# Linear attention and a gated feed-forward block: first queries in 1 KB runs, the sums of batch 0's second half behind the first half-units, batch 1's squares shared between two engines, and the steady groups' sums in consecutive units

## The chip, the cores and the metric

The kernel runs on one core of one Trainium2 chip. The metric is device time in microseconds (us). The time of an execution is about 2 us more than the span of its profile (325.02 us against a span of 323.1 us for the profiled run of the kernel before).

Names of the engines in the profile: PE is TensorE (matrix products), PEld its weight loads, DVE is VectorE, ACT is ScalarE, POOL is GpSimd, SP is SyncE, which here only issues DMAs. "SPq" and "ACTq" are those engines' sequencers.

## The reference, cut to what matters

```python
# q, k, v: [8 batches, 8 heads, 576 rows, 64], float32
kv  = einsum('bhsd,bhse->bhde', k, v)           # 64 x 64 state of each head
out = einsum('bhsd,bhde->bhse', q, kv)
out = out / sqrt(mean(out*out, -1) + 1e-6) * g_norm
x   = out.transpose(0, 2, 1, 3).reshape(4608, 512)
xn  = x / sqrt(mean(x*x, -1) + 1e-6) * rms_g
y   = (silu(xn @ w_gate) * (xn @ w_val)) @ w_out   # 512 -> 1536 -> 512
```

Both norms are folded into one scale per row and head, "alpha", made of two sums over the squares of a head: a plain one and one weighted by the square of `g_norm`.

## The kernel before

Batch by batch, 512 rows of each batch form a group: 12 "up" units (a gate product, a value product, SiLU, multiplication), then the "down" products. The last 64 rows of all eight batches form a ninth group. While PE runs one group's feed-forward, the next batch's attention is slipped in between the units. The order on each engine is the program's order.

Batch 0 has no predecessor to hide behind. It is done in two halves of 256 rows, called A and Z: load queries, cast, turn (transpose) on PE, column products, squares, sums, root, scaling, turn, and then the first up units, in half and quarter sizes:

```python
def load_q0(f, hs, queue):                       # f: half of the 512 rows
    src = q[0, hs, 256*f : 256*f+256, :].rearrange("h (p t) d -> p h (t d)", t=2)   # runs of 512 B
    queue.dma_start(out=q0[:, f, hs, :], in_=src)

def put_q0(f, ps, half, engine):                 # turned queries, PSUM -> SBUF
    js = slice(2*half, 2*half+2)
    cast(engine, qt0[:, js, 256*f : 256*f+256], ps[:, js].rearrange("p j i t -> p j (i t)"))
...
    A.sums()
    oA = rows_of(A)
    cast_q0(1, hs0, DVE)
    cast_q0(1, hs1, GP)
    A.head()
    qps = turn_q0(1, 0)
    A.root_by_table(lambda: put_q0(1, qps, 0, DVE))
    put_q0(1, qps, 1, SC)
    ...                                          # block 0 weights rounded, Z's columns and squares
    xs = [A.scale(c, oA[c]) for c in range(2)]
    x_turn(A, 0, xs[0], DVE)
    x_turn(A, 1, xs[1], DVE)
    Z.alloc_sums()
    Z.sums()

    ffn = Ffn(0)
    first = ffn.pair_banks()
    for lo in (0, 128):
        for u in range(2):
            ffn.half_unit(first[0], u, wg_sb, u, lo, lo + 128)
    oZ = rows_of(Z)
    for u in range(2):
        ffn.half_unit(first[1], u, wv_sb, u, 0, 256)
    Z.head()
    Z.root_by_table(lambda: round_w(1, "g", 2, DVE))
    ...
    xs = [Z.scale(c, oZ[c]) for c in range(2)]
    for s, engine in enumerate((GP, SC, DVE, DVE)):
        round_w(1, "v", s, engine)               # "rounding": scale a weight slice, write it as bf16
    SC.preload_act_table(ACT.Silu)
    clear_tail_rows(0, GP)                       # two memsets of 64 x 512
```

Batch 1 takes its sums from squares of columns, and batches 2 to 7 spread theirs over the steps of the running group:

```python
def f_cols(j):
    ...
    F.turned(j, ps)
    SC.activation(out=F.sq[:, j, :], in_=ps, func=ACT.Square)

# steady groups: step u runs after up unit u of group n
kv0, os = (2, (4, 5, 7, 8)) if n == 1 else (0, (2, 4, 6, 7))
for c, u in enumerate(os):
    steps[u].append(lambda a=a, c=c: a.o(c))           # products, squares
    steps[u + 1].append(lambda a=a, c=c: a.sums(c))    # VectorE
late = int(n == 1)
steps[9 + late]  += [a.head]
steps[10 + late] += [a.guess]
steps[11] += [a.root]
for c in range(T):
    steps[11] += [lambda a=a, c=c: a.scale(c), lambda a=a, c=c: a.x_rows(c)]  # x_rows: DMA transpose
```

## Time and profile before

| | |
|---|---|
| time | 325.02 us median of 3 runs (324.85 to 325.19) |
| PE busy | 315.9 us of a span of 323.1 us |
| one 512-column product | 216 ns from start to start |
| PE stretches with waits | 0 to 22 us, 40.2 us (0.18 us, which the prediction did not list), 48.8 us, 122.3 us |

The page of the kernel before, its line of busy times (us, share of the span, instructions) and the line of the chain that ended last, by engine:

```profile
PE 315.9 (98%) x1925; PEld 156.8 (49%) x1925; DVE 180.9 (56%) x370; ACT 178.1 (55%) x318; POOL 21.2 (7%) x44
...
PE 85%; DMA 7%; DVE 4%; SPq 1%; ACT 1%; issue 1%; DVEq 0%
```

PE is full except at the start and in a few short waits. The chain of waits of the kernel before for its first 50 us shows what the start is made of. Columns: start in us, length in us, what.

```profile
1.64 6.53 DMA st<-in_q_dram
...
9.30 9.27 DMA st<-in_moe_w_gate_dram
...
18.59 0.35 DVE wg_sb L203
18.95 0.17 DVE Zal L449
...
19.21 1.29 DVE xna L453 x2
20.50 0.90 DVE wv_sb L203 x2
...
21.45 0.72 PE v_ps L489 x5
```

The load of the first queries, then the load of the second block of gate weights, then VectorE: a rounding, the reciprocal that ends Z's root (`Zal`), two scalings, two roundings, for which PE waits. The timeline of the kernel before shows that last wait. Columns: start, length, engine, line, operation, out<-in, shape, count, and in brackets the idle time before.

```profile
20.42 0.97 DVE L203 TENSOR_SCALAR wv_sb<-st,rowscale 128x256 bf16<-128x256 f32 x2
20.70 0.55 POOL L280 MEMSET kb<- 64x512 bf16 x1
20.79 0.49 PE L489 MATMUL v_ps<-xnt,wv_sb 128*128 128x256 bf16 x3
21.18 0.67 POOL L280 MEMSET vb<- 64x512 bf16 x1
21.45 0.72 PE L489 MATMUL v_ps<-xnt,wv_sb 128*128 128x256 bf16 x5 [0.17 <-DVE wv_sb L203]
```

From the third to the fourth of these products 440 ns pass instead of 109: 0.33 us lost. The two roundings together take 0.97 us.

Batch 1's sums in the timeline of the kernel before:

```profile
48.37 0.62 ACT L856 ACTIVATE sqt<-v_ps 128x512 bf16<-128x512 f32 x1
...
48.52 0.78 PE L419 MATMUL att_ps<-sel,sqt 128*128 128x4 bf16 x16
49.04 0.17 PEld L419 LDWEIGHTS <-sqt 128*128 128x128 bf16 x4 [0.17 <-ACT sqt L856]
```

The last four sums wait for ScalarE's last square; by the starts of the products, 0.22 us are lost. The third group's border in the timeline of the kernel before:

```profile
114.69 5.17 SPq L385 DMA_TRANSPOSE xnt<-xna  x4
...
122.79 1.03 PE L472 MATMUL g_ps<-xnt,wg_sb 128*128 128x512 bf16 x4 [0.25 <-DMA xnt<-xna]
```

The four transposes of the next x are issued from 114.69 us on; the last one, issued at 118.63 us, lands at 122.75, and 0.41 us are lost by the starts of the products.

### The profile page before, as it was taken

To read this page: it belongs to the slowest core of one execution; us is meant where nothing else is said; L and a number is where in the kernel's file an instruction comes from. 1 tells how busy PE (TensorE), PEld (TensorE's weight loads), DVE (VectorE), ACT (ScalarE), POOL (GpSimd) and SP (SyncE) were. 2 spreads that over 40 slices of the span, in tenths; PEclk is the share of its full clock that TensorE was granted. 3 is DMA by queue.
4 is the path that set the end of the run, shared out by engine and by line. 5 is a ranking of instruction groups with operands and counts; after the bars stand their busy time and mean duration, and the time that the engine had idled before them with its cause. 6 is when DMAs were issued, how large, how long until landed. Compare 5 with 4: busy or idle time off the path is not lost.

```text
span 323.1 us, 5133 instructions
## 1 busy us (share of the span) xinstructions
PE 315.9 (98%) x1925; PEld 156.8 (49%) x1925; DVE 180.9 (56%) x370; ACT 178.1 (55%) x318; POOL 21.2 (7%) x44
## 2 busy tenths in 40 slices
PE   8899999999999999999999999999999999999995
PEld 3585455554454444444544454444544444444443
DVE  4786747569437942785268615870588058803410
ACT  3586547666756575557665765666554355223321
POOL 1263252100000000000000000000000000000000
PEclk9999999999999999999999999999999999999999
DMA  7999999994379556942794279956101620050014
GB/s 258 349 350 386 379 373 290 258 295 127 65 193 291 137 66 178 309 134 51 193 307 134 48 148 201 314 140 162 66 2 26 152 83 0 18 169 12 0 35 97
DMA packets 75125, 54.87 MB, mean 170 GB/s; under 512 B 42200, under 2 KB 68060, under 8 KB 75100
## 3 DMA queue, kind: packets, MB, share of 16 engines
q1 hardware_dynamic: 74720, 53.88, 59.5%
q10 hardware_dynamic: 380, 0.66, 0.6%
q8 instruction: 15, 0.25, 0.3%
q14 instruction: 10, 0.08, 0.1%
HBM read 37.75 MB, written 9.44 MB: 146 GB/s over the span
## 4 chain that ended last, share of the span: by engine, by line
PE 85%; DMA 7%; DVE 4%; SPq 1%; ACT 1%; issue 1%; DVEq 0%
PE g_ps L472 27%; PE v_ps L472 27%; PE o_ps L516 23%; DMA st<-in_moe_w_gate_dram 3%; PE att_ps L272 2%; DMA st<-in_q_dram 2%; PE att_ps L343 2%; DMA xnt<-xna 1%; DVE h_sb L478 1%; DVE xna L378 1%; PE g_ps L516 1%; PE v_ps L516 1%; DMA out_dram<-o_sb 1%; ACT sqt L856 1%; SPq L385 1%
## 5 line engine op out<-in xcount | busy, mean ns | idle before, releaser
L478 DVE TENSOR_TENSOR h_sb<-silu,v_ps 128x512 bf16<-128x512 bf16 x104 | 71.1, 683 | 109.8 <-PE v_ps L472 72.7
L472 PE MATMUL g_ps<-xnt,wg_sb 128*128 128x512 bf16 x416 | 106.8, 380 | 0.2 <-DMA xnt<-xna 0.2
L472 PE MATMUL v_ps<-xnt,wv_sb 128*128 128x512 bf16 x416 | 106.8, 379 | 0.0
L477 ACT ACTIVATE silu<-g_ps 128x512 bf16<-128x512 f32 x104 | 62.6, 602 | 63.4 <-PE g_ps L472 55.4
L516 PE MATMUL o_ps<-wo_sb,h_sb 128*128 128x512 bf16 x396 | 87.5, 379 | 0.0
L472 PEld LDWEIGHTS <-wv_sb 128*128 128x128 bf16 x416 | 40.7, 98 | 49.1
L516 PEld LDWEIGHTS <-h_sb 128*128 128x128 bf16 x420 | 40.7, 98 | 47.8 <-issue 0.2
L472 PEld LDWEIGHTS <-wg_sb 128*128 128x128 bf16 x416 | 38.6, 98 | 40.5 <-DMA xnt<-xna 0.7
L106 ACT COPY o_sb<-o_ps 128x512 f32<-128x512 f32 (+1 forms) x34 | 19.7, 580 | 38.1 <-PE o_ps L516 37.3
L361 DVE TENSOR_REDUCE ssq<-sq 128x16 f32<-128x1024 bf16 x28 | 34.2, 1220 | 1.0
L352 ACT ACTIVATE sq<-att_ps 128x512 bf16<-128x512 f32 x28 | 16.7, 597 | 13.7 <-PE att_ps L343 8.7
L106 ACT CAST vb<-st 128x512 bf16<-128x512 f32 (+2 forms) x33 | 18.9, 625 | 5.2 <-DMA st<-in_v_dram 5.2
L378 DVE TENSOR_TENSOR xna<-outa,s1y 128x512 bf16<-128x512 bf16 x28 | 17.5, 686 | 0.2
L106 ACT CAST qb<-st 128x1024 bf16<-128x1024 f32 (+1 forms) x15 | 14.2, 987 | 3.8 <-DMA st<-in_q_dram 3.8
L354 ACT CAST outa<-att_ps 128x512 bf16<-128x512 f32 x28 | 16.3, 581 | 0.0
L106 ACT CAST kb<-st 128x512 bf16<-128x512 f32 (+1 forms) x25 | 14.0, 619 | 0.0
L360 DVE TENSOR_TENSOR sq<-sq,gsq 128x512 bf16<-128x512 bf16 x28 | 11.7, 419 | 0.0
L343 PEld LDWEIGHTS <-qt 128*128 128x128 bf16 x96 | 7.4, 98 | 5.7
L343 PE MATMUL att_ps<-kv_all,qt 128*128 128x128 bf16 x96 | 9.3, 219 | 0.0
L272 PEld LDWEIGHTS <-kb 128*128 128x128 bf16 x120 | 7.7, 98 | 2.8
L613 PE MATMUL att_ps<-kv_all 128*128 128x512 bf16 (+1 forms) x21 | 7.5, 486 | 1.2 <-DVE sel L602 1.2
L272 PE MATMUL att_ps<-vb,kb 128*128 128x128 bf16 x120 | 8.7, 219 | 0.0
(137 smaller groups left out, 167.2 us busy)
## 6 DMA issues: line engine op xcount, KB each, us to landing
out_dram<-o_sb SPq DMA_DIRECT2D x16, 512.0 KB, 3.0
st<-in_q_dram SPq DMA_DIRECT2D x7, 1024.0 KB, 7.2
st<-in_k_dram SPq DMA_DIRECT2D x6, 1024.0 KB, 10.3
st<-in_v_dram SPq DMA_DIRECT2D x6, 1024.0 KB, 10.9
st<-in_moe_w_out_dram SPq DMA_DIRECT2D x6, 512.0 KB, 12.2
st<-in_moe_w_gate_dram SPq DMA_DIRECT2D x4, 512.0 KB, 9.3
st<-in_moe_w_val_dram SPq DMA_DIRECT2D x4, 512.0 KB, 9.9
st<-in_k_dram SPq DMA_DIRECT2D x4, 288.0 KB, 5.1
```

Source lines behind the costliest of these rows:

```text
L106: engine.copy(out=dst, in_=src)
L272: PE.matmul(ps, lhsT=bufs[b]["k"][:, t, hs, :], rhs=bufs[b]["v"][:, t, hs, :], start=(first and t == 0), stop=(last and t == T),)
L343: PE.matmul(cols, lhsT=self.qt[:, j, 128 * c : 128 * c + 128], rhs=kv_all[:, self.n, j, :], start=(j == 0), stop=(j == NS - 1),)
L352: SC.activation(out=self.sq[c][:, 0], in_=ps, func=ACT.Square)
L354: SC.copy(out=self.outa[c], in_=ps)
L360: DVE.tensor_tensor(out=sq[:, 1], in0=sq[:, 0], in1=gsq8, op=OP.mult)
L361: DVE.reduce_sum(out=self.ssq[:, c], in_=sq, axis=AX.X)
L378: DVE.tensor_tensor(out=self.xna[c], in0=self.outa[c], in1=self.alpha[:, c, :].to_broadcast([128, H, D]), op=OP.mult)
L472: PE.matmul(ps, lhsT=wt[:, s, j * 128 : (j + 1) * 128], rhs=x[:, s, :], start=(s == 0), stop=(s == NS - 1),)
L477: SC.activation(out=silu, in_=g_ps, func=ACT.Silu)
L478: DVE.tensor_tensor(out=self.h[:, j, :], in0=silu, in1=v_ps, op=OP.mult)
L516: PE.matmul(self.o_ps[c], lhsT=self.h[:, j, c * 128 : (c + 1) * 128], rhs=wo_sb[:, j, :], start=(j == 0), stop=(j == NF - 1),)
```

## The change

The intent: fewer, longer transfers for the first queries, so that batch 0 starts sooner; the squares of batch 1 off ScalarE's critical piece; and x of the steady groups ready one or two units sooner. A partition now takes 4 rows of 4 heads in 1,024 B runs, alternate partitions holding the two groups of heads; copies with a stride of 2 separate them after the turn, both of them on ScalarE for the second half. Besides, the sums of Z, which stood in front of the first half-units of the feed-forward, now stand behind the first two of them. The rows of batch 0 therefore leave in another order, in four DMAs instead of two.

```diff
+            elif c % 2 == 1 and n == 0:
+                r0 = 256 * (c // 2)
+                rows = out[r0 : r0 + 256, :].rearrange("(p c t) d -> t p c d", c=2, t=2)
+                for t in range(2):
+                    nc.sync.dma_start(out=rows[t], in_=self.o_sb[64 * t : 64 * t + 64])
...
-    def load_q0(f, hs, queue):
-        src = q[0, hs, 256 * f : 256 * f + 256, :].rearrange("h (p t) d -> p h (t d)", t=2)
-        queue.dma_start(out=q0[:, f, hs, :], in_=src)
+    def load_q0(f, queue):
+        dst = q0[:, f].rearrange("(p g) h x -> p g h x", g=2)
+        for g in range(2):
+            src = q[0, 4 * g : 4 * g + 4, 256 * f : 256 * f + 256, :].rearrange("h (p t) d -> p h (t d)", t=4)
+            queue.dma_start(out=dst[:, g], in_=src)
...
+        return ps.rearrange("p j t (x g) -> p j t x g", g=2)
+    def put_q0(f, ps, g, engine):
+        dst = qt0[:, 2 * g : 2 * g + 2, 256 * f : 256 * f + 256].rearrange("p j (t x) -> p j t x", t=4)
+        cast(engine, dst, ps[:, :, :, :, g])
...
-    A.root_by_table(lambda: put_q0(1, qps, 0, DVE))
-    put_q0(1, qps, 1, SC)
+    A.root_by_table(lambda: None)
+    for g in range(2):
+        put_q0(1, qps, g, SC)
...
-    Z.alloc_sums()
-    Z.sums()
     ffn = Ffn(0)
     first = ffn.pair_banks()
+    Z.alloc_sums()
     for lo in (0, 128):
         for u in range(2):
             ffn.half_unit(first[0], u, wg_sb, u, lo, lo + 128)
+        if lo == 0:
+            Z.sums()
...
-        SC.activation(out=F.sq[:, j, :], in_=ps, func=ACT.Square)
+        if j == 1:
+            copy = osb_pool.tile([128, 2, d_model], FP32, name="o_sb")[:, 0, :]
+            DVE.tensor_copy(out=copy, in_=ps)
+            DVE.tensor_tensor(out=F.sq[:, j, :], in0=copy, in1=ps, op=OP.mult)
+        else:
+            SC.activation(out=F.sq[:, j, :], in_=ps, func=ACT.Square)
...
     att1.kv_copy()
+    clear_tail_rows(1, DVE)
+    for i, engine in enumerate((DVE, SC, DVE, GP)):
+        cast_q(1, slice(2 * i, 2 * i + 2), engine)       # both stood elsewhere before
...
-            kv0, os = (2, (4, 5, 7, 8)) if n == 1 else (0, (2, 4, 6, 7))
+            kv0, os = (2, (4, 5, 7, 8)) if n == 1 else (0, (2, 3, 5, 6))
...
-            late = int(n == 1)
-            steps[9 + late] += [a.head]
-            steps[10 + late] += [a.guess]
-            steps[11] += [a.root]
+            late = 2 * int(n == 1)
+            steps[8 + late] += [a.head]
+            steps[9 + late] += [a.guess, a.root]
             for c in range(T):
-                steps[11] += [...]
+                steps[10 if c == 0 and not late else 11] += [...]
```

More of the change, by code (lines that the diff above doesn't have):

```diff
@@ L531, in down_out @@
                     )
-            elif c % 2 == 1:
-                if n == 0:
-                    r0 = 256 * (c // 2)
-                    rows = out[r0 : r0 + 256, :].rearrange("(p t) d -> p t d", t=2)
-                else:
-                    rows = out[n * S : n * S + MAIN, :].rearrange("(p t) d -> p t d", t=T)[:, c - 1 : c + 1, :]
+            elif c % 2 == 1 and n == 0:
[3 more added lines that the diff above has]
+                    nc.sync.dma_start(out=rows[t], in_=self.o_sb[64 * t : 64 * t + 64])
+            elif c % 2 == 1:
+                rows = out[n * S : n * S + MAIN, :].rearrange("(p t) d -> p t d", t=T)[:, c - 1 : c + 1, :]
                 nc.sync.dma_start(out=rows, in_=self.o_sb)
@@ L573 @@
         alloc_kv(0, name)
-    q0 = stage().rearrange("p (f h x) -> p f h x", f=2, h=H)
-    def load_q0(f, hs, queue):
-        src = q[0, hs, 256 * f : 256 * f + 256, :].rearrange("h (p t) d -> p h (t d)", t=2)
-        queue.dma_start(out=q0[:, f, hs, :], in_=src)
+    q0 = stage().rearrange("p (f h x) -> p f h x", f=2, h=H // 2)
+    def load_q0(f, queue):
[3 more added lines that the diff above has]
+            queue.dma_start(out=dst[:, g], in_=src)
     for j in (0, 1):
@@ L588 @@
     )
-    load_q0(0, slice(0, 8), nc.sync)
+    load_q0(0, nc.sync)
     for j in (2, 3):
@@ L592 @@
         load_kv(0, "v", nc.sync, slice(j, j + 1))
-    load_q0(1, slice(0, 8), nc.sync)
+    load_q0(1, nc.sync)
     for blk in range(2):
@@ L623 @@
     Z = Cols(0, 256, 512, qt0, sqt0, "Z")
+    qb0 = qb0.rearrange("p t h d -> p (t h d)").rearrange("p (f t h d) -> p f t h d", f=2, t=4, h=4)
     def cast_q0(f, hs, engine):
-        cast(engine, qb0[:, 2 * f : 2 * f + 2, hs, :], q0[:, f, hs, :].rearrange("p h (t d) -> p t h d", t=2))
+        cast(engine, qb0[:, f, :, hs, :], q0[:, f, hs, :].rearrange("p h (t d) -> p t h d", t=4))
     def turn_q0(f, dummies):
@@ L630, in turn_q0 @@
         warm(bank, dummies)
-        ps = bank.bitcast(BF16).rearrange("p (j i t) -> p j i t", j=NS, i=2)
-        for j in range(NS):
-            for i in range(2):
+        ps = bank.bitcast(BF16).rearrange("p (j t x) -> p j t x", j=2, t=4)
+        for j in range(2):
+            for t in range(4):
                 PE.matmul(
-                    ps[:, j, i, :], lhsT=qb0[:, 2 * f + i, 2 * j : 2 * j + 2, :], rhs=identity,
-                    is_transpose=True, start=(i == 0 and j == 0), stop=(i == 1 and j == NS - 1),
-                )
-        return ps
-    def put_q0(f, ps, half, engine):
-        js = slice(2 * half, 2 * half + 2)
-        cast(engine, qt0[:, js, 256 * f : 256 * f + 256], ps[:, js].rearrange("p j i t -> p j (i t)"))
+                    ps[:, j, t, :], lhsT=qb0[:, f, t, 2 * j : 2 * j + 2, :], rhs=identity,
+                    is_transpose=True, start=(j == 0 and t == 0), stop=(j == 1 and t == 3),
+                )
+        return ps.rearrange("p j t (x g) -> p j t x g", g=2)
+    def put_q0(f, ps, g, engine):
+        dst = qt0[:, 2 * g : 2 * g + 2, 256 * f : 256 * f + 256].rearrange("p j (t x) -> p j t x", t=4)
+        cast(engine, dst, ps[:, :, :, :, g])
     def state0(j, dummies):
@@ L678, in rows_of @@
         return banks
-    hs0, hs1 = slice(0, 4), slice(4, 8)
+    hs0, hs1 = slice(0, 2), slice(2, 4)
     warm_ps = att_pool.tile([128, 512], FP32, name="att_ps")
@@ L693 @@
     put_state0(1, kv1)
+    banksA = [gps_pool.tile([128, MAIN], FP32, name="g_ps"), vps_pool.tile([128, MAIN], FP32, name="v_ps")]
     qps = turn_q0(0, 2)
@@ L706 @@
     cast_kv(0, "v", 3, DVE)
-    banksA = [gps_pool.tile([128, MAIN], FP32, name="g_ps"), vps_pool.tile([128, MAIN], FP32, name="v_ps")]
     columns(A, 0, banksA[0])
@@ L729 @@
     A.head()
+    banksZ = [gps_pool.tile([128, MAIN], FP32, name="g_ps"), vps_pool.tile([128, MAIN], FP32, name="v_ps")]
     qps = turn_q0(1, 0)
-    A.root_by_table(lambda: put_q0(1, qps, 0, DVE))
-    put_q0(1, qps, 1, SC)
+    A.root_by_table(lambda: None)
+    for g in range(2):
+        put_q0(1, qps, g, SC)
     for name in ("g", "v"):
@@ L736 @@
                 round_w(0, name, s, GP)
-    banksZ = [gps_pool.tile([128, MAIN], FP32, name="g_ps"), vps_pool.tile([128, MAIN], FP32, name="v_ps")]
     warm(banksZ[0], 2)
@@ L847 @@
         round_wo(0, i, 1, engine)
-    for i, engine in enumerate((DVE, SC, DVE, GP)):
-        cast_q(1, slice(2 * i, 2 * i + 2), engine)
     alloc_xnt(1)
@@ L882 @@
             round_wo(blk, i, 1, GP)
-    clear_tail_rows(1, GP)
     F = Cols(1, 0, 512, turns.qt, sqt_pool.tile([128, NS, MAIN], BF16, name="sqt"), "F")
@@ L967 @@
                 steps[u + 1].append(lambda a=a, c=c: a.sums(c))
-            late = int(n == 1)
-            steps[9 + late] += [a.head]
-            steps[10 + late] += [a.guess]
-            steps[11] += [a.root]
+            late = 2 * int(n == 1)
+            steps[8 + late] += [a.head]
+            steps[9 + late] += [a.guess, a.root]
             for c in range(T):
-                steps[11] += [lambda a=a, c=c: a.scale(c), lambda a=a, c=c: a.x_rows(c)]
+                steps[10 if c == 0 and not late else 11] += [lambda a=a, c=c: a.scale(c), lambda a=a, c=c: a.x_rows(c)]
         b = n + 2
```

## The prediction

> **What bounds it.** TensorE: the page has PE busy for 315.9 of 323.1 us at full clock, and the table of stretches 20.00 of 20.00 us almost everywhere after 60 us; a 512-column product takes 216 ns. The change keeps every TensorE instruction, so it can win only PE idle time. By the starts of consecutive products in the timeline that lies in three places:
> - 0 to 22 us. The chain of waits: the query load (1.64 to 8.17 us), the gate-weight load (9.30 to 18.57), VectorE work behind it, the last value-weight rounding, for which PE waits 0.33 us at 21.0. DMA share: 0.98 in the first 20 us, 1.06 in the next.
> - Batch 1's sums at 48.8 us: 0.22 us for ScalarE's last of four column squares (597 ns each).
> - The border at 122.3 us: 0.4 us, until the group's last transposed x tile lands (122.75). Other borders lose under 0.1.
>
> **Costs and gains.**
> 1. Query load. Packets: 512 B take about 29 ns, 1,024 B about 51. Estimate: 2,048 small packets are 59 us of engine time, 1,024 larger ones 52; over 16 engines 0.4 us less. The Trainium skill (DMA: Bandwidth & Descriptors, Specifications) gives 512 B as the least transfer for line rate; this trace disagrees (17.6 against 20 B/ns per engine). The extra issues also hold the second half until the first has landed, so v's last piece (11.22 us) competes with less. The load stream up to 43 us moves 0.4 us forward.
> 2. Strided copies. VectorE's copy of a turned half was 0.42 us. The Trainium skill (VectorE: DVE Perf Modes, What auto-detection actually checks) wants 16-bit operands at step 1 for the fast mode; at step 2 I expect 0.68 us, as 512 fp32 elements from PSUM take here. ScalarE stays at 0.58. Off the critical path: the last pair's k and v products end later.
> 3. Z's sums later: no PE work saved. A's chain may come 0.6 us forward; Z's root still waits for weights and VectorE, so 0.4 is left at 21.5 us.
> 4. Batch 1: VectorE takes one column's copy and product (about 0.68 us each) while idle. Wins 0.2. Clearing tail rows and later query casts hide behind the query load landing at 43.17 us; that has 0.3 us to spare, so PE cannot come much further forward than the loads.
> 5. Steady groups: head, guess and root one to two units earlier from batch 3 on. PE is full; VectorE (11 of 20 us) has room. Only the 122.3 us border wins, 0.4. Batch 2's border at 89.2 us stays just in time.
> 6. Batch 0's output in four issues, not two: transposes of batch 2's queries about 0.4 us later, with 0.8 to spare.
>
> **Prediction.** 0.4 + 0.2 + 0.4, about 1.0 to 1.1 us less: **323.9 us**, 80% range 323.0 to 324.8. Faster by over 2%: 0.01; within 2%: 0.98; slower by over 2%: 0.01.
>
> **What would show it.** First query half landing at 7.5 to 7.9 us instead of 8.18, the last v piece by 10.7; first full-width up product at about 25.4 instead of 25.9; no wait before batch 1's sums; no gap at the third border; strided VectorE copy near 0.68 us.
>
> **What would make it wrong.** Loads into every other partition slower than 20 B/ns; the load pace past 20 us not following, so that PE waits at batch 1's query turn (gain only 0.5); the first stage gaining its whole 0.6 us or more (gain 1.5); a new wait at the 89 us border; VectorE's longer runs of sums holding up an up unit.

## The result, and the profile after

| | changed kernel | kernel before | ratio, 95% interval |
|---|---|---|---|
| first measurement | 324.70 us (324.46 to 324.87, 4 runs) | 325.11 us (324.85 to 325.56, 4 runs) | 0.9985 [0.9968, 1.0003] |
| again, another chip | 324.62 us (323.99 to 325.01, 6 runs) | 325.25 us (324.89 to 325.86, 11 runs) | 0.9975 [0.9963, 0.9987] |

A ratio is the mean time of one kernel's fast runs over that of the other's of the same rounds, so not quite the ratio of the medians quoted beside it. The gain is 0.4 to 0.6 us where 1.0 to 1.1 was forecast: the time is inside the forecast range, but the gain is about half of what the terms add up to, and the interval of the first measurement still holds 1.

The page of the changed kernel, the same two lines:

```profile
PE 316.0 (98%) x1925; PEld 156.5 (49%) x1925; DVE 181.5 (56%) x373; ACT 178.3 (55%) x318; POOL 20.3 (6%) x42
...
PE 92%; DMA 4%; DVE 2%; SPq 0%; ACT 0%; issue 0%; DVEq 0%
```

To see where the time came from, I lay the two traces side by side at five points, each the start of one instruction in the timeline (us):

| point | before | after | difference | second pair: before, after, difference |
|---|---|---|---|---|
| scaling of A's rows starts | 15.15 | 14.81 | -0.34 | 15.73, 15.02, -0.71 |
| first SiLU of a full-width unit | 26.89 | 27.21 | +0.32 | 27.12, 27.60, +0.48 |
| first SiLU of group 1 | 57.26 | 57.16 | -0.10 | 57.50, 57.76, +0.26 |
| first SiLU of group 4 | 157.61 | 157.11 | -0.50 | 157.78, 157.72, -0.06 |
| end of the span | 323.06 | 322.65 | -0.41 | 323.17, 323.21, +0.04 |

The second pair is a slower-than-usual execution of the changed kernel (325.01 us, the slowest of its six) against a usual one of before (325.15), so its end is no measure of the gain; its course is what matters. In both pairs the changed kernel comes earlier into A's scaling and **later** out of the first stage. It then wins back what it lost at other places. In the first pair these are 0.18 us at a hold at 40.2 us that the changed kernel happened not to have (its second profile has it), 0.22 us at batch 1's sums and 0.41 us at the third border; in the second pair 0.22 and 0.24 us.

The chain of waits of the changed kernel, first 30 us:

```profile
1.64 5.06 DMA st<-in_q_dram
...
7.37 5.50 DMA st<-in_q_dram
...
12.97 0.43 DVE qb L108
13.40 0.18 DVE Ar L224
...
17.66 0.27 DVE Zr L224
...
18.53 0.35 DVE wg_sb L203
18.88 0.20 DVE Zal L449
...
19.17 1.29 DVE xna L453 x2
20.46 0.99 DVE wv_sb L203
...
21.50 0.99 PE v_ps L489 x6
```

The two parts of the first query half land at 6.70 and 7.44 us (before, the whole at 8.18), and those of the second half are issued at 6.72 and 7.37. A's sums run at 12.41 us instead of 13.18, but A's head (`Ar`) stands in VectorE's order behind the cast of the second query half (12.97 us), so only 0.31 of these 0.77 us remain: 13.31 instead of 13.62. Then Z's chain begins (`Zr`, its first reciprocal) at 17.66 instead of 17.35 us. In the chain of before, the load of the second gate block (landing at 18.57 us) ended last, and VectorE's rounding of it (`wg_sb`) followed at 18.59. Here this load lands at 18.18 us, but VectorE, busy with Z's chain, comes to the rounding only at 18.45, so at the end of Z's root (`Zal`) 0.04 us is left of the load's 0.39: 18.82 instead of 18.86 in the timelines. And the last rounding stands there with 0.99 us alone. The timeline of the changed kernel at that place:

```profile
20.30 0.52 POOL L280 MEMSET kb<- 64x512 bf16 x1
20.38 1.33 DVE L203 TENSOR_SCALAR wv_sb<-st,rowscale 128x256 bf16<-128x256 f32 x2
20.75 0.38 PE L489 MATMUL v_ps<-xnt,wv_sb 128*128 128x256 bf16 x2
20.76 0.53 POOL L280 MEMSET vb<- 64x512 bf16 x1
...
21.50 0.99 PE L489 MATMUL v_ps<-xnt,wv_sb 128*128 128x256 bf16 x6 [0.36 <-DVE wv_sb L203]
```

The single records of the two roundings are 1,060 and 347 ns. The first began 0.08 us after the first memset and ended 0.15 us after the second one. PE loses 0.53 us before its third product and 0.16 before its fourth, where before it lost 0.33.

Batch 1's sums in the timeline of the changed kernel run through without a wait (0.55 us for the sixteen, before 0.78); VectorE's copy and product take 0.69 us each:

```profile
47.99 0.69 DVE L864 TENSOR_TENSOR sqt<-o_sb,att_ps 128x512 bf16<-128x512 f32 x1
48.02 0.60 ACT L866 ACTIVATE sqt<-v_ps 128x512 bf16<-128x512 f32 x1
...
48.64 0.55 PE L419 MATMUL att_ps<-sel,sqt 128*128 128x4 bf16 x16
```

At the third border of the changed kernel the transposes go out 1.83 us sooner and PE does not wait:

```profile
112.86 5.16 SPq L385 DMA_TRANSPOSE xnt<-xna  x4
...
122.30 1.03 PE L472 MATMUL g_ps<-xnt,wg_sb 128*128 128x512 bf16 x4
```

### The profile page after: what moved, and what is told of

It reads as the page before. It is cut to its first block, busy times and chain, and to the rows that moved or that the text cites. A ratio compares the mean times of both kernels' runs of the same rounds, so it can differ in the third digit from the quotient of the medians.

```text
span 322.7 us, 5143 instructions
## 1 busy us (share of the span) xinstructions
PE 316.0 (98%) x1925; PEld 156.5 (49%) x1925; DVE 181.5 (56%) x373; ACT 178.3 (55%) x318; POOL 20.3 (6%) x42
## 4 chain that ended last, share of the span: by engine, by line
PE 92%; DMA 4%; DVE 2%; SPq 0%; ACT 0%; issue 0%; DVEq 0%
PE g_ps L472 28%; PE v_ps L472 28%; PE o_ps L516 27%; DMA st<-in_q_dram 3%; PE att_ps L272 2%; PE att_ps L343 2%; PE v_ps L516 1%; PE g_ps L516 1%; DVE xna L453 1%; DMA out_dram<-o_sb 1%; PE v_ps L489 1%; PE o_ps L489 1%; PE g_ps L489 0%; PE att_ps L338 0%; PE att_ps L285 0%; PE att_ps L265 0%
## 5 line engine op out<-in xcount | busy, mean ns | idle before, releaser
L360 DVE TENSOR_TENSOR sq<-sq,gsq 128x512 bf16<-128x512 bf16 x28 | 11.7, 418 | 0.0
## 6 DMA issues: line engine op xcount, KB each, us to landing
st<-in_moe_w_out_dram SPq DMA_DIRECT2D x6, 512.0 KB, 11.4
```

Source lines behind the costliest of these rows:

```text
L360: DVE.tensor_tensor(out=sq[:, 1], in0=sq[:, 0], in1=gsq8, op=OP.mult)
```

## The experiments

Two theories stood for the loss in the first stage. **P**: GpSimd's two memsets of batch 0's tail rows, which now begin just as VectorE's last roundings do, hold these roundings up. **Z**: Z's sums, now behind the first half-units, start Z's root, scaling and roundings too late. All kernels below gave correct results. Times are against the kernel before in the same rounds.

Because loads land at other times in each execution (in the nine profiles of kernels that share the changed kernel's code up to Z's sums, the second gate block landed between 17.46 and 19.28 us), single profiles are compared by two things that need no common clock: the length of the two roundings, and the stretch from the start of A's scaling to the first SiLU of a full-width unit. I collect them here from the records:

```
kernel              roundings (ns)   PE gaps (us)   stretch (us)
before               365   689       0.33            11.74
before_again         345   697       -               11.39
after               1060   347       0.53 + 0.16     12.40
after_again          366   689       0.33            12.58
late_clear           421   333       -               11.70
double_clear         872   690       0.34 + 0.50     12.51
z_sums_first         345   692       -               11.43
z_late               366   337       -               11.27
z_late_cast          346   348       -               11.29
before_late_clear    362   334       -               11.66
before_z_later      1231   346       0.70 + 0.16     12.47
query_only           365   347       -               11.22
undo_f               344   575       0.19            11.86
undo_steady          448   333       -               11.73
```

(PE gaps: time beyond the usual 109 ns from one product to the next within the second pair's eight value products, where it is over 0.15 us.)

Two things stand in these rows beside the theories. First, the memsets are not alone: the 421, 448 and 575 ns of late_clear, undo_steady and undo_f overlap no memset but a weight rounding that GpSimd does itself (20.93 to 21.41, 21.11 to 21.59 and 21.05 to 21.68 us), and end 0.14 to 0.15 us after it. Second, whether VectorE's roundings meet the memsets changes from one execution to the next: after, after_again, undo_f and undo_steady have the same code up to there, and lose 0.69, 0.33, 0.19 (none of it to a memset) and 0 us.

### late_clear: the memsets elsewhere

```diff
-    clear_tail_rows(0, GP)
     ...
     for s in (2, 3):
         round_w(4, "v", s, GP)
+    clear_tail_rows(0, GP)
```

> The changed kernel, with GpSimd's two clearings of batch 0's tail rows (two memsets of 64x512) moved from about 20.3 us to after the last weight roundings. Theory P: VectorE's last value-weight roundings are held while a GpSimd memset runs (1.06 us for the first one in the changed kernel, 0.36 us when undisturbed). Then both roundings take about 0.36 us, the gap before PE's third product of the second value pair falls from 0.53 to under 0.1 us, and the first full-width up product comes at about 25.6 instead of 26.1 us; about 0.4 to 0.5 us faster than the changed kernel (which is about 0.4 faster than before), so 0.8 to 0.9 under before. Theory Z: the loss is due to Z's sums standing behind the first half-units, so the roundings start too late: then nothing moves by more than 0.1 us.

Measured: 324.65 us (324.23 to 325.03, 5 runs), before 325.01; ratio 0.9988 [0.9974, 1.0002]. Its timeline:

```profile
21.14 0.68 DVE L203 TENSOR_SCALAR wv_sb<-st,rowscale 128x256 bf16<-128x256 f32 x2
21.51 0.97 PE L489 MATMUL v_ps<-xnt,wv_sb 128*128 128x256 bf16 x7
```

The two roundings take 0.68 us together, PE runs through, and the stretch is 0.70 us shorter than in the first profile of the changed kernel (undo_steady, whose memsets end before the roundings begin, has 11.73 us without any such move). That is what theory P said of the mechanism. The time did not follow: it is that of the changed kernel. Three things are visible. The profiled execution had late loads (v's last piece cast at 11.75 us, against 10.47 in the first profile of the changed kernel), so 27.3 us was no earlier than there; that speaks of the profile, not of the median of five runs. The changed kernel does not lose its 0.69 us to the memsets in every execution (above). And the new place of the memsets, 33 us, was badly chosen, as before_late_clear shows below. How much each counts in the median is not shown. My expectation of 0.4 to 0.5 us in time failed.

### double_clear: the memsets twice

```diff
-    clear_tail_rows(0, GP)
+    for _ in range(2):
+        clear_tail_rows(0, GP)
```

> The changed kernel with the two clearings of batch 0's tail rows done twice on GpSimd (the result is the same). Theory P: the roundings of value weights wait for four memsets instead of two, about 1.0 us more, and the first full-width up product comes about 0.9 us later (27.0 us). Theory Z: GpSimd is not on the chain, nothing moves by more than 0.2 us.

Measured: 324.84 us (324.66 and 325.01, 2 runs), before 325.01; ratio 0.9994 [0.9976, 1.0012]. Its timeline:

```profile
19.86 0.52 POOL L280 MEMSET kb<- 64x512 bf16 x1
20.12 1.48 DVE L203 TENSOR_SCALAR wv_sb<-st,rowscale 128x256 bf16<-128x256 f32 x2
20.32 0.53 POOL L280 MEMSET vb<- 64x512 bf16 x1
...
20.78 0.67 POOL L280 MEMSET kb<- 64x512 bf16 x1
...
21.66 0.72 PE L489 MATMUL v_ps<-xnt,wv_sb 128*128 128x256 bf16 x5 [0.33 <-DVE wv_sb L203]
```

Both roundings are now held (872 and 690 ns, the two PE gaps 0.84 us together), but not by all four memsets: the second rounding gets its turn after the third memset. So my size for theory P (1.0 us more) was wrong. A rounding waits for the memsets that are running or already in line, one or two of them, and ends about 0.15 us after the last of these; then the engines take turns. The third and fourth memset, which met a waiting rounding, took 0.67 and 0.66 us instead of 0.52.

### z_sums_first: Z's sums back in front

```diff
     ffn = Ffn(0)
     first = ffn.pair_banks()
-    Z.alloc_sums()          # and Z.sums() out of the loop over lo
+    # Z.alloc_sums() and Z.sums() stand before these two lines, as before the change
```

> The changed kernel with Z's sums back in front of the first half-units. Theory Z: the reciprocal of Z's chain starts at about 17.2 instead of 17.66 us, Z's scaling and the roundings behind it 0.3 to 0.4 us sooner, the first full-width up product at 25.7 to 25.8; about 0.4 us faster than the changed kernel. Theory P: the chain starts sooner but the last rounding still ends only when GpSimd's memsets do (21.3 us), so the gain is under 0.2 us.

Measured: 324.08 us (323.39 to 324.49, 5 runs), before 325.01; ratio 0.9970 [0.9957, 0.9983]. Its timeline:

```profile
16.86 0.26 DVE L224 RECIPROCAL Zr<-att_ps 128x16 f32<-128x16 f32 x1
...
19.58 0.96 DVE L203 TENSOR_SCALAR wv_sb<-st,rowscale 128x256 bf16<-128x256 f32 x2
...
20.21 1.10 PE L489 MATMUL v_ps<-xnt,wv_sb 128*128 128x256 bf16 x8
```

Z's chain starts at 16.86 us, and everything behind it is 0.8 us sooner than in the first profile of the changed kernel. Not all of that is the order, since A's scaling is 0.20 us earlier here too. The fairer twin is double_clear, which has the later order and the same loads: its A's scaling starts at 14.60 us (here 14.61), its second gate block lands at 17.72 (17.71), and Z's chain in its timeline starts here:

```profile
17.41 0.26 DVE L224 RECIPROCAL Zr<-att_ps 128x16 f32<-128x16 f32 x1 [0.60 <-PE att_ps L419]
```

That is 0.55 us later, and Z's scaling is still 0.54 us later (18.91 against 18.37): the later sums cost this much on the chain, before any memset is met. With the sums in front, Z's chain is early enough that the load ends last again (the rounding of the second gate block starts at 17.73 us, 0.02 after its landing). The second rounding is still held (692 ns), but PE comes to it late enough not to lose anything. The first SiLU of a full-width unit comes at 26.04 us against 27.21, and 0.6 of these 1.2 us reach the end of the span (322.07 against 322.65); 0.4 us go into a hold at 39.2 us: by the records, batch 1's 19th column product starts 402 ns after the 18th, right behind VectorE's cast of the last pieces of v, where in the changed kernel's first profile it starts at once. The time is 0.5 to 0.6 us under that of the changed kernel (324.08 against 324.62 and 324.70). Its interval lies clear of 1, but that compares it with before; it overlaps those of the changed kernel. The closest comparison in time is with late_clear and double_clear, timed on the same chip in the same rounds with the later order: their seven runs are 0.66 us slower in the mean (95% interval about 0.1 to 1.2). On the other chip z_late and z_late_cast together are 0.39 us faster than after_again (about -0.1 to 0.9). So the order's cost is shown on the chain (0.54 us); in time it is likely, and its size is uncertain.

### z_late and z_late_cast: both mends, and one cast moved

z_late is z_sums_first with late_clear. z_late_cast has, besides:

```diff
-    cast_q0(1, hs0, DVE)
+    cast_q0(1, hs0, SC)
```

> The changed kernel with both mends: Z's sums in front of the first half-units and the memsets moved to about 33 us. From the start of A's scaling to the first full-width gate activation: 12.4 us in the changed kernel, 11.7 with the memsets late, 11.4 with Z's sums first. If the two causes add: 11.1 or less, and the time 0.8 to 1.2 us under before, part of the gain going into the wait for batch 1's k and v casts at 39 us (0.4 us with Z's sums first alone). If only one of them counts: as Z's sums first alone (0.9 us under before).

> As the one with both mends, and the first four heads of the second query half cast by ScalarE instead of VectorE, so that A's head needs not stand behind that cast in VectorE's order. A's head starts at about 12.8 instead of 13.1 to 13.3 us where the second half lands at 12.9. If A's chain is what holds the dense products: another 0.3 us faster. If Z's chain is (second query half, its copies, squares, sums): the first full-width product and the time stay within 0.15 us of the one with both mends.

Measured: z_late 323.71 us (323.49 to 325.19, 6 runs), before 325.25; ratio 0.9965 [0.9947, 0.9984]. z_late_cast 324.10 us (323.75 to 324.96, 6 runs); ratio 0.9967 [0.9954, 0.9980]. The stretch is 11.27 and 11.29 us. By the stretches, order alone is worth 11.70 - 11.27 = 0.43 us (late_clear against z_late) and the memsets are worth 0.70 us with the sums behind the half-units (12.40 - 11.70), but only 0.16 us with the sums in front (11.43 - 11.27). These are differences of single profiles whose loads differ, so they are rough; what they suggest is that the two causes do not add, because the earlier chain also steps out of the memsets' way. z_late is the fastest kernel by its median, but two of its six runs were at 325.0 and 325.2 at full clock, and its interval overlaps that of z_sums_first; I do not claim a difference between these two.

Moving the cast to ScalarE changed nothing that can be told apart. In z_late's profile the second query half happened to land early (12.66 us), so A's head was not held there either. Moreover z_late's chain of waits runs over the second gate block's load (landing at 17.74 us, its rounding on VectorE from 17.77), so an earlier head of A could not have helped. The test of the cast's place in the order is inconclusive.

### before_late_clear and before_z_later: the same two steps without the rest

The first is the kernel before with the memsets moved as in late_clear; the second is the kernel before with Z's sums moved as in the change.

> The kernel before, with only the clearing of batch 0's tail rows moved to about 33 us. Theory P: the second of VectorE's value roundings (0.69 us in both profiles of before, inside a memset) takes 0.35 us, and where a PE gap of 0.33 us stood before the fourth product of the second value pair it closes; up to 0.3 us faster than before, less where VectorE's chain is late enough anyway (no such gap in the second profile of before).

> The kernel before, with only Z's sums moved behind the first two half-units. From A's scaling to the first full-width gate activation took 11.7 and 11.4 us in before. If the order alone costs: the reciprocal of Z's chain comes about 0.45 us later and this stretch grows to 11.8 to 12.4 us; 0.3 to 0.5 us slower than before. If the later sums only cost together with the query part (its two copies one after the other): no change over 0.1 us.

Measured: before_late_clear 325.19 us (324.88 to 325.41, 5 runs), before 325.17; ratio 0.9996 [0.9984, 1.0008]. before_z_later 325.23 us (325.17 to 325.42, 4 runs); ratio 1.0000 [0.9987, 1.0013].

The timeline of before_z_later has the collision at its worst:

```profile
20.49 1.50 DVE L203 TENSOR_SCALAR wv_sb<-st,rowscale 128x256 bf16<-128x256 f32 x2
20.58 0.52 POOL L280 MEMSET kb<- 64x512 bf16 x1
...
21.77 0.77 PE L489 MATMUL v_ps<-xnt,wv_sb 128*128 128x256 bf16 x4 [0.53 <-DVE wv_sb L203]
```

In this profile the roundings take 1,231 and 346 ns instead of 365 and 689, and the stretch 12.47 us instead of 11.4 to 11.7, without any of the query part. So the query part is not needed for the collision. But this is one profile, and how much of it is the order's doing is not shown: the second gate block landed at 18.45 us and was rounded at 18.56, so the later order can have held Z's chain up by 0.11 us at most, and Z's scaling, at 19.28 us, is no later than in before (19.21 and 19.46); GpSimd's memset came 0.12 us earlier than in before (20.58 against 20.70), and a shift of about 0.1 us decided the meeting. In this execution, then, the load hides nearly the whole cost of the later order. In time it shows nothing, against my 0.3 to 0.5 us. Two other things differ as well: the hold of 0.2 us that before has ahead of batch 1's 19th column product (203 ns from the 18th, at 40.2 us) is gone here, and this kernel's loads were among the earlier ones (A's scaling at 15.03 us).

In before_late_clear the roundings are 362 and 334 ns and the gap of 0.33 us is gone, as expected, and the time stays. The list of what PE waited for, of that kernel (us in total, times, longest):

```profile
PE v_ps L472 <- DVE wv_sb L203: 0.4, 1, 0.4
```

That wait is new: at 33 us VectorE rounds the last block's value weights (0.83 and 0.82 us; in before 0.85 and 0.47), and the memsets I had moved there (32.90 and 33.52 us) hold the second of them; by the starts of the products PE loses 0.52 us. z_late has the same wait, 0.42 us, late_clear 0.20. So my mend put the collision in another place. That covers the 0.33 us won in before_late_clear; in late_clear it covers only a part. A place where VectorE does no rounding, or VectorE itself, would be the next thing to try.

### query_only: the first part alone

The kernel before with the load, casts, turns and outputs of the change, the second half's copies by VectorE and ScalarE as before; orders of sums, batch 1 and the steady groups as before.

> The kernel before with only the query part: 1 KB runs, strided copies (the second half's by VectorE and ScalarE as before), four output issues, PSUM banks of the columns taken earlier. If the load part gives what the landing times of the other profiles say (gate weights of block 1 at 17.7 to 18.2 instead of 18.6 to 18.8 us): 0.4 to 0.7 us faster than before, with the gap before batch 1's sums (0.2 us) still there. If the strided copies or the half-partition loads take it back: within 0.2 us of before.

Measured: 324.84 us (324.12 to 325.63, 6 runs), before 325.17; ratio 0.9986 [0.9974, 0.9999]. The gate weights of block 1 landed at 17.40 us, against 18.45 to 18.82 in the four profiles of kernels with the old load. The gap before batch 1's sums is there (0.22 us). But there was no gap at the third border, although the steady groups are in the old order: see below. VectorE's strided copy took 0.69 us and stood before the reciprocal that ends A's root: from A's head to that reciprocal 1.52 us passed, against 1.25 before and 1.15 in the changed kernel, which gives both copies to ScalarE. By these single profiles that move is worth 0.37 us on A's chain.

### undo_steady, before_again, after_again: what closed the third border

undo_steady is the changed kernel with the steady groups' orders as before; the other two are second profiles of the two kernels.

> The changed kernel with the order of sums, head, guess, root and scale of the steady groups as in the kernel before. If the border at 122 us was won by this part, a PE gap of about 0.4 us returns there (last transposed x tile landing after the last down product), and nothing else changes: 0.4 us slower than the changed kernel, so about equal to before. If the border was won by loads that come at other times, the gap does not return.

> The kernel before, once more, for a second profile. Undoing the steady part did not bring the gap at the third border back; in the first profile of before some transfers of the last transpose took 1.6 us, others about 50 ns. Theory 'chance': this profile shows no gap over 0.1 us there, and the last x tile lands within 2.6 us of its issue. Theory 'order': the old order makes the gap each time, 0.4 us again. The roundings of the second value pair: one or both over 0.6 us if they meet a GpSimd memset.

> The changed kernel, once more, for a second profile and more times on one chip. About 0.4 us under before. Theory P: its two value roundings take 0.35 us each where they start after the memsets' end, and 0.6 to 1.1 us where they start inside; the PE gap before the third product of the second value pair follows that. If the first stage's start differs by chance, second query half landing between 12.2 and 13.4 us.

Measured: undo_steady 324.75 us (324.31 to 325.07, 4 runs), before 325.01; ratio 0.9991 [0.9977, 1.0004]. Its timeline, with the transposes as late as before:

```profile
115.25 5.15 SPq L385 DMA_TRANSPOSE xnt<-xna  x4
...
122.58 1.03 PE L472 MATMUL g_ps<-xnt,wg_sb 128*128 128x512 bf16 x4
```

No gap. before_again has it: 0.24 us, its last tile landing 3.95 us after its issue. So neither "order" nor "chance" is right. The trace's DMA records say what it is:

```
                 fetch of 16,384 B      last x transpose:   its packets of 256 or 4 B
                 start     length       issued              longest     over 500 ns
before           119.66    1573 ns      118.63              1659 ns     16
before_again     119.89    1512 ns      118.96              1511 ns     16
query_only       123.10     964 ns      118.52                53 ns      0
undo_steady      123.97     947 ns      119.18               249 ns      0
after            121.32    1062 ns      116.81                56 ns      0
```

Each kernel fetches 16,384 B of its own program by DMA every 11 to 26 us (queue 8, kind "instruction" in the DMA table). In all four profiles with the old query part (these two, 0.28 us in before_late_clear, 0.29 in before_z_later) this fetch begins 0.9 to 1.2 us after the last transpose's issue, and 15 or 16 of the transpose's small packets, median 18 ns, take 1.4 us and more beside it. In all ten profiles with the new query part the fetch begins 4.3 to 4.8 us after that issue, and PE has no gap. No run moves the fetch alone, so this cause is read from the records (four profiles against ten) and not shown by an experiment. The program that is fetched is another one (four more DMA issues, among others); what sets the moment of the fetch I did not find. Whether the steady part alone, with the old query part, would have closed the gap is not shown: no run has it.

after_again's roundings were 366 and 689 ns, with a gap of 0.33 us. Its loads were the latest of all (second gate block at 19.28 us).

### undo_f: batch 1's squares back on ScalarE

> The changed kernel with batch 1's squares all on ScalarE, tail rows cleared by GpSimd and query casts ahead of the state's copy, as before. The PE gap of 0.2 us before the last of batch 1's sums returns; 0.2 us slower than the changed kernel. If instead ScalarE was not what the sums waited for, no gap comes and the time stays.

Measured: 324.84 us (324.55 to 325.43, 4 runs), before 325.17; ratio 0.9988 [0.9974, 1.0003]. Its timeline:

```profile
48.84 0.78 PE L419 MATMUL att_ps<-sel,sqt 128*128 128x4 bf16 x16
49.36 0.17 PEld L419 LDWEIGHTS <-sqt 128*128 128x128 bf16 x4 [0.16 <-ACT sqt L863]
```

The gap of 0.22 us returns exactly. The run puts three things back at once (the squares, the clearing of tail rows, the query casts), but what the view names as ending the wait is ScalarE's square. In time 0.2 us is within the noise of these rounds, so the trace is the evidence here.

## Why the prediction was right or wrong

The kernel stays within 2% and the time within the range, so the outcome was right. By its terms it was 0.4 + 0.2 + 0.4, and it measured 0.4 to 0.6 in all. That it lies in the range is partly luck: the first term came out negative (about -0.3 us in the first pair of profiles), the third came from something that was not foreseen, and the range ended only 0.2 us under the time of before (324.8 against 325.02).

1. **Query load: right for the first half and the weights, and larger than estimated in its typical size.** 1,024 B packets took 48 to 51 ns on average against 29 to 30 for 512 B. The first half landed at 7.44 us (forecast 7.5 to 7.9), the last v piece at 10.45 (10.7). But over the ten profiles with the new load that v piece landed between 10.45 and 11.87 us, over the four with the old between 10.89 and 11.81: that it comes earlier is not shown. The second gate block landed at 17.4 to 18.2 us in nine of the ten profiles with the new load, and at 19.28 in one, against 18.45 to 18.82 in the four with the old. The prediction took one execution's landing times as fixed; they move by 0.7 us and more between executions of the same instructions.
2. **Strided copies: right.** 0.69 us by VectorE, 0.68 forecast, 0.42 before; 0.58 by ScalarE as before. They cost nothing that can be seen: from A's sums to Z's sums 3.81 us pass in z_sums_first, 3.78 in before.
3. **Z's sums later: this is the step that failed.** The prediction said "Z's root still waits for weights and VectorE, so 0.4 is left at 21.5 us", and the first full-width product at about 25.4 instead of 25.9 us. In its place that product came at 26.14 us (before 25.82), and the changed kernel came out of the first stage 0.32 and 0.48 us *later* than before. Two things made the difference. First, the weights were no longer what Z's root waited for last. Their load came 0.39 us sooner, as forecast, but the later sums hold Z's chain up by 0.54 us (z_sums_first against double_clear), and so the chain, being nearly all on VectorE, ended last: 0.04 us was left at `Zal`. Second, VectorE's roundings met GpSimd's memsets (themselves 0.40 us earlier, since the value weights land earlier), for PE gaps of 0.69 us in the first profile. In the second profile (after_again) the load, landing at 19.28 us, did end last, so its 0.48 us are in part a late load. With the sums left in front, the rest of the change gives 0.9 us over before (z_sums_first, 325.01 to 324.08), close to the forecast sum. The Trainium skill (SBUF — State Buffer, Who interferes with whom) states that VectorE in its two-port modes and GpSimd exclude each other for a whole instruction and that tensor_scalar can enter these modes; traces agree, with 333 to 366 ns for a rounding that is hardly held or not at all, 689 to 1,231 ns for one that meets one or two memsets, and 421 to 575 ns for one that meets a rounding of GpSimd's. I read that page only after the result.
4. **Batch 1's sums: right**, 0.22 us, shown in the traces by undo_f and query_only, which have the gap, against the changed kernel, which has not.
5. **Steady groups: right number, wrong cause.** The border's gap (0.24 to 0.41 us over four profiles) closed. But it closed in query_only and undo_steady too, with the old order. By the DMA records it came from a program fetch that held up the last transpose's packets; with the query part that fetch falls at another moment. I had read "waits for the last transpose" as "the transpose is issued too late", without asking why that transpose took 4.1 us and its neighbours 2.4.
6. **Four output issues: right.** No new wait of PE between 56 and 122 us.

A term that the prediction lacked: the hold ahead of batch 1's 19th column product, behind VectorE's cast of v. It is 203 ns in before, nothing in the first profile of the changed kernel and in before_z_later, 226 ns in the second profile of the changed kernel, 402 ns in z_sums_first and 95 ns in z_late. Roughly, a chain that comes sooner meets more of it, so it swallows part of what the first stage gains; but the two profiles of the changed kernel differ by as much, and no run isolates it.

Left open: how much that hold takes in a typical execution; why two of z_late's runs were 1.4 us slower; whether A's head behind the query cast matters where the second query half lands late; and what decides when a program fetch falls.

## What to carry to other kernels

When a chain of small steps on one engine is the critical path, moving its first step behind "free" work on another engine costs the full delay wherever no other wait ends later (0.54 us in double_clear; at most 0.11 in before_z_later, where a load ended at nearly the same time); before moving it, follow the chain to the end and ask which other instruction it will then meet. Compare single records of the same instruction and shape: one that takes twice as long as its twin has met something, and that is worth finding before anything is predicted. And when a transfer ends a wait, compare its own duration with its neighbours' before concluding that it was started too late.

## What the Trainium skill lacked or had wrong

- DMA: Bandwidth & Descriptors, Specifications, gives 512 B as the least transfer for line rate. Here, from HBM into SBUF in the first 14 us, 512 B packets took 29 to 30 ns on average (17 to 17.5 B/ns per engine), 1,024 B packets 48 to 53 ns (19 to 21), and 2,304 B packets 102 to 110 ns (21 to 23): by these times 512 B is not yet at the full rate.
- DMA: Bandwidth & Descriptors, Queues, rings and completion order, says that an engine takes turns between queues and where program refills run, but not what a fetch costs the others: here, at the third border, a fetch of 16,384 B took 0.9 to 1.6 us and ran on a queue that the trace numbers 8 (the page names row 14 for refills; the trace has fetches of up to 8,192 B on a queue 14 too), and beside it 15 or 16 packets of 256 or 4 B, otherwise 18 ns, took up to 1.66 us.
- SBUF — State Buffer, Who interferes with whom, has the exclusion of VectorE and GpSimd right, but not the size that a chain pays: a VectorE tensor_scalar of 128x256 (333 to 366 ns when hardly held or not at all) took 689 to 697 ns against one 64x512 memset and 872 to 1,231 ns against two in a row, and 421 to 575 ns against a rounding of GpSimd's, ending about 0.15 us after the end of GpSimd's instruction; the memset that met it took 0.67 instead of 0.52 us.
- No page says how far the first loads vary between executions of the same instructions: the second gate block landed between 17.46 and 19.28 us over nine profiles.
